# Two products of the next pair among the output steps of a pair, in a hand-ordered convolution and SwiGLU kernel

## The chip, the cores and the metric

The kernel runs on one core of one Trainium2 chip. The metric is the device time of one execution in microseconds (us), as the median of the executions shown. The profiler's trace of one further execution stands beside it, with times from the first to the last instruction (the span).

## The reference

The input `x` holds 8 sequences of 4096 tokens with 192 values each. First comes a causal convolution over 7 tokens, with one softmax-normalised set of 7 taps for each of 8 heads (24 values a head); then, token by token, an RMS norm and a gated feed-forward layer with 1536 hidden values, all in fp32:

```
out = einsum('hk,bskhg->bshg', softmax(weight), windows of x)   # lightweight_conv
rms = sqrt(mean(out * out) + 1e-6);  xn = out / rms * rms_g
g = xn @ w_gate;  silu = g / (1 + exp(-g));  val = xn @ w_val
result = (silu * val) @ w_out                                    # 32768 x 192
```

## The kernel before, in words

**Tiling.** The 32768 tokens are cut into 32 *pairs* of two tiles of 512 tokens. Pair 0 and pair 1 are made in a prologue with plain fp32 products (lines 881 and 1090), while weights are prepared. Pairs 2 to 31 run in a steady order that repeats once a pair; a *window* is one such repeat (the loop over `w` at the end of the kernel).

**Products.** The hidden values of a pair come from *products* (`product`, matmul at line 909). One product is six matmuls of 64 rows by 128 columns over 512 tokens: three parts of a split operand, each for the gate (array rows 0 to 63) and the value (rows 64 to 127) at once, so a product is three concurrent matmul couples. Left operands are pieces of the split weights, loaded from DRAM into a ring of 10 slots (`ring_load`, line 789, queue of SyncE); the right operands are five groups of split token sums. The 12 blocks of 128 hidden values are taken as 6 couples `j`, each with four cells a, b, c, d (two token tiles by two blocks), each cell a double bank of PSUM (gate and value). For `j` = 1 and 3 each cell gets three products of its own (named A, B, E with the cell: `Ab.1`). For `j` = 0, 2, 4, 5 a Winograd-like form needs 11 products (P1 to P7, Q1 to Q4) and sums in between. So a pair has 4x11 + 2x12 = 68 products.

**Emptying the banks.** The order is written out as words: engine letter (V VectorE, A ScalarE, G GpSimd, S the DMA queue of SyncE), act, index. `f1.j` copies cell a into a new bank b, `f3.j` copies c to SBUF (both line 674 on ScalarE, line 676 on VectorE), `f4.j` and `f5.j` add the copy to b (VectorE, line 980; f5 opens cell d). `ga` to `gd` take the SiLU of a gate bank (ScalarE, line 986), `ma` to `md` multiply by the value bank (VectorE, line 993) and so write the hidden values `ht`. A bank is free for another cell when both have read it. There are four double banks for everything.

**Output.** `h1.k` to `h4.k` are sums of hidden values in place (line 963, VectorE or GpSimd, SBUF to SBUF). An output step `oF.k` (form F of 1 to 7, k of 0 to 5; `step`, matmul at line 936) is a set of matmuls with tiles of 128 rows by 32 columns, in plain fp32. The 42 steps add into accumulators X (forms 1, 6, 5, 3), Y (2) and Z (7, 4), of one double bank each. `c1` copies X into Y, `s7` and `c2` copy Z and X to SBUF, `C22` and `C21` (line 1010) add X and Z to these copies, `T11`, `T12`, `T21`, `T22` (line 951) transpose into `o_sb`, and `Sst` stores it (line 1042). `C22` must read X before the steps of form 3 add to it; `T12` reads X after them.

**Next pairs, meanwhile.** `cv0` to `cv6` are the taps of a convolution (lines 440 to 444), `sq`, `red`, `pow`, `bc`, `mul` the norm (`mul` on GpSimd, line 494), `Spl`, `Sft`, `Sld` DMAs that put the result away, fetch it transposed and load the next tokens; `x1` to `x4` (line 831), `n` (ScalarE, line 674), `l` (line 817) and `d` (line 819) make the five groups of split operands (0 to 4) of the next pair.

**What sets the order.** `ORDER` holds the words of a window: `pN` lets TensorE take N further products or steps of the window's pair from `LINE`; a suffix `-` means the pair before, `+` and `++` the next and the one after. Every engine keeps its own queue in that order, and semaphores hold an instruction until what it reads is there, or its bank is free. `FIRST` is the window of pair 1, with the preparation of the split weights (`W`) in it. In the kernel before, `LINE` starts a pair with P1.0 P5.0 Ab.1 P6.0 Bb.1 Eb.1 P7.0 P3.0 Q2.0 P2.0 Q1.0 Q4.0, and all 42 output steps of a pair stand behind its 68 products and ahead of the next pair's first product; 15 of these steps stand at the start of the next window.

Of the kernel before, what the change touches and what calls it, by code (L numbers as in the profile page):

```python
# [20 lines left out]
def kernel(  # L21
# [55 lines left out]
        "a5 b5 c5 d5",  # L77
    )
    ORDER = (
# [14 lines left out]
    )  # L94
    FIRST = (
# [13 lines left out]
    )  # L109
    LINE = (  # L110
# [7 lines left out]
    )  # L118

    cst = ctx.enter_context(tc.tile_pool(name="cst", bufs=1))  # L120
# [1176 lines left out]
```

## Time and profile before

| what | value |
|---|---|
| time, median of 3 (lowest to highest) | 2484.42 us (2483.5 to 2485.6) |
| the profiled execution: its own time, its span | 2486.79 us, 2485.0 us |
| granted TensorE clock | 0.999 |
| VectorE, ScalarE, GpSimd busy | 2051.4, 993.1, 795.2 us |
| HBM read, written | 366.96 MB, 58.98 MB |

In the page's rows PE is the matmul part of TensorE and PEld its weight loads, DVE is VectorE, ACT ScalarE, POOL GpSimd, and SPq and ACTq are DMA queues. A group's row gives line, engine, operation, tiles and shape, count, then busy us and mean ns of one, then the engine's idle time before it with the releaser. A timeline row gives start, length, engine, line, operation, tiles and count; in square brackets stands the idle time before it and what ended it. A row of waits gives the total, the number and the longest.

### The profile page before, as it was taken

What the parts mean: (1) busy time and instruction counts of PE and PEld (TensorE: products, weight loads), DVE (VectorE), ACT (ScalarE), POOL (GpSimd) and SP (SyncE); (2) the same over time, 40 slices, a digit from 0 to 9 for tenths busy, and PEclk for the clock granted to TensorE, in tenths of its full rate; (3) what the DMA queues carried; (4) which work ended last, traced back from release to release, by engine and by line L of the source; (5) the groups of instructions that cost most, each with busy time, mean ns of one, the idle gap of its engine ahead of it and who ended that gap; (6) DMA issues with size and microseconds to landing.
All of it is one profiled execution on the core that took longest, in us unless ns stands there. A gap on an engine that the chain in (4) does not pass through costs nothing.

```text
span 2485.0 us, 69316 instructions
## 1 busy us (share of the span) xinstructions
PE 2464.4 (99%) x29152; PEld 1923.9 (77%) x29152; DVE 2051.4 (83%) x2614; ACT 993.1 (40%) x1405; POOL 795.2 (32%) x566
## 2 busy tenths in 40 slices
PE   8999999999999999999999999999999999999998
PEld 5547778878787777788887778877788777888876
DVE  8688888888888888888888888888887888888864
ACT  6443334434344434344334343333344343444332
POOL 0541332323332323323323324233423233333222
PEclk9999999999999999999999999999999999999999
DMA  6364678666677666787667786666776666776653
GB/s 151 60 205 127 167 182 211 178 172 168 170 193 198 179 165 171 175 204 185 182 161 175 179 206 185 173 164 172 187 200 185 171 168 170 199 192 186 161 159 92
DMA packets 716392, 430.55 MB, mean 173 GB/s; under 512 B 510330, under 2 KB 702386, under 8 KB 716082
## 3 DMA queue, kind: packets, MB, share of 16 engines
q1 hardware_dynamic: 712336, 425.21, 66.6%
q8 instruction: 230, 3.77, 0.6%
q10 hardware_dynamic: 3746, 0.92, 0.2%
q14 instruction: 80, 0.66, 0.1%
HBM read 366.96 MB, written 58.98 MB: 171 GB/s over the span
## 4 chain that ended last, share of the span: by engine, by line
PE 94%; DVE 2%; DMA 1%; SPq 1%; issue 1%; POOL 0%; ACT 0%; DVEq 0%; POOLq 0%
PE ps L909 57%; PE ps L936 35%; PE ps L881 2%; DMA ht<-in_moe_w_gate_dram 0%; SPq L237 0%; DVE ht L1108 0%; DVE ht L963 0%; SPq L153 0%; DVE y L444 0%; DMA xb<-xd 0%; DMA x<-in_x_dram 0%; DMA hs<-in_moe_w_out_dram 0%; DVE part L344 0%; DMA ring<-wd 0%; POOL part L335 0%
## 5 line engine op out<-in xcount | busy, mean ns | idle before, releaser
L909 PE MATMUL ps<-part,ring 64*128 64x512 f32 x12240 | 1434.0, 390 | 2.6 <-DVE ps L980 0.4
L909 PEld LDWEIGHTS ps<-part,ring 64*128 64x128 f32 x12240 | 1174.3, 184 | 255.3 <-DVE ps L980 32.3
L986 ACT ACTIVATE tt<-ps 128x512 f32<-128x512 f32 x744 | 436.1, 599 | 714.4 <-PE ps L909 636.0
L993 DVE TENSOR_TENSOR ht<-ps,tt 128x512 f32<-128x512 f32 x744 | 495.5, 686 | 195.6 <-ACT tt L986 192.4
L936 PE MATMUL ps<-ht,wo_sb 128*32 128x384 f32 (+2 forms) x7272 | 471.6, 380 | 0.8 <-POOL wo_sb L336 0.8
L963 POOL TENSOR_TENSOR ht<-ht 128x512 f32<-128x512 f32 x182 | 279.0, 1563 | 568.7 <-PE ps L936 568.7
L936 PE MATMUL ps<-ht,x 128*32 128x256 f32 (+2 forms) x6696 | 429.1, 379 | 1.3 <-DVE ht L963 1.3
L936 PEld LDWEIGHTS ps<-ht,wo_sb 128*32 128x32 f32 x7272 | 332.4, 110 | 102.4 <-DVE tt L831 9.4
L980 DVE TENSOR_TENSOR ps<-ps,tt 128x1024 f32<-128x1024 f32 x240 | 295.6, 1232 | 97.8 <-ACT tt L674 55.6
L936 PEld LDWEIGHTS ps<-ht,x 128*32 128x32 f32 x6696 | 299.0, 110 | 87.5 <-DVE ht L963 2.0
L444 DVE SCALAR_TENSOR_TENSOR y<-xh,tp,y 128x1536 f32<-128x1536 f32 x186 | 338.9, 1822 | 2.5 <-ACT y L440 2.3
L674 ACT COPY ps<-ps 128x1024 f32<-128x1024 f32 (+1 forms) x151 | 134.0, 887 | 478.6 <-PE ps L909 367.9
L963 POOL TENSOR_TENSOR hs<-ht 128x512 f32<-128x512 f32 x120 | 165.5, 1390 | 405.2 <-DVE ht L993 405.2
L473 POOL TENSOR_SCALAR r<-r 128x8 f32<-128x8 f32 x31 | 6.1, 198 | 484.5 <-DVE r L468 484.4
L674 ACT COPY tt<-ps 128x1024 f32<-128x1024 f32 (+1 forms) x152 | 121.6, 800 | 68.7 <-PE ps L936 57.9
L963 DVE TENSOR_TENSOR ht<-ht 128x512 f32<-128x512 f32 x190 | 132.5, 698 | 9.7 <-PE ps L936 6.4
L936 PE MATMUL ps<-hs,x 128*32 128x128 f32 (+2 forms) x2232 | 130.1, 379 | 0.0
L936 PEld LDWEIGHTS ps<-hs,x 128*32 128x32 f32 x2232 | 94.0, 110 | 30.7
L674 ACT CAST part<-tt 128x1024 fp32r<-128x1024 f32 x60 | 62.9, 1049 | 136.8 <-DVE tt L831 136.8
L963 DVE TENSOR_TENSOR ht<-hs,ht 128x512 f32<-128x512 f32 x156 | 106.7, 729 | 1.2 <-PE ps L936 0.6
L819 DVE SCALAR_TENSOR_TENSOR part<-part,xb 128x1024 fp32r<-128x1024 f32 x87 | 105.9, 1218 | 0.0
L817 POOL TENSOR_TENSOR part<-xb,part 128x1024 fp32r<-128x1024 f32 x29 | 96.6, 3329 | 0.0
(131 smaller groups left out, 1436.5 us busy)
## 6 DMA issues: line engine op xcount, KB each, us to landing
ring<-wd SPq DMA_DIRECT2D x1440, 192.0 KB
xb<-xd SPq DMA_DIRECT2D x60, 512.0 KB
xd<-xh SPq DMA_DIRECT2D x240, 96.0 KB
xh<-in_x_dram SPq DMA_DIRECT2D x192, 105.0 KB
xb<-xd SPq DMA_DIRECT2D x60, 256.0 KB
out_dram<-o_sb SPq DMA_DIRECT2D x126, 96.0 KB
out_dram<-o_sb SPq DMA_DIRECT2D x62, 128.0 KB
wd<-part SPq DMA_DIRECT2D x5, 1152.0 KB
```

What stands on the lines that cost most here:

```text
L444: nc.vector.scalar_tensor_tensor(out=y, in0=xk, scalar=w, in1=y, op0=ALU.mult, op1=ALU.add)
L473: nc.gpsimd.tensor_scalar(out=r, in0=r, scalar1=s / D, scalar2=s * 1e-6, op0=ALU.mult, op1=ALU.add)
L674: nc.scalar.copy(out=dst, in_=src)
L817: e.tensor_tensor(out=split_of(g, 1).bitcast(F32R), in0=src, in1=high, op=ALU.subtract)
L819: nc.vector.scalar_tensor_tensor(out=split_of(g, 2).bitcast(F32R), in0=high, scalar=1.0 + SPLIT, in1=src, op0=ALU.mult, op1=ALU.subtract,)
L881: nc.tensor.matmul(out=self.both(j, c)[:, h, :], lhsT=wf[HALF[h], k, 2 * HOME[j] + f, :], rhs=rb[HALF[h], k, g, :], start=(k == 0), stop=( ...
L909: nc.tensor.matmul(out=self.both(j, c)[:, h, :], lhsT=left[HALF[h]], rhs=right[HALF[h]], start=(first and q == 0), stop=True, skip_group_c ...
L936: nc.tensor.matmul(out=self.acc(b)[i * Q : (i + 1) * Q, at : at + n], lhsT=left, rhs=cols, start=fresh, stop=True, skip_group_check=True, ...
L963: engine[eng].tensor_tensor(out=dst, in0=a, in1=b, op=op)
L980: nc.vector.tensor_tensor(out=self.both(j, c), in0=self.both(j, "b"), in1=s5, op=ALU.add)
L986: nc.scalar.activation(out=tt[:, t, :], in_=self.both(j, c)[:, 0, :], func=AF.Silu)
L993: nc.vector.tensor_tensor(out=self.hv(j, "abcd".index(c)), in0=self.both(j, c)[:, 1, :], in1=tt[:, t, :], op=ALU.mult,)
```

## The change

Three strings of words are replaced; no instruction of the arithmetic is added or dropped. These are the last part of `LINE` and the seam of `ORDER` (a window's end and, in the next round, its start), cut to what is spoken of:

```diff
 LINE, first and last rows
-        "P1.0 P5.0 Ab.1 P6.0 Bb.1 Eb.1 P7.0 P3.0 Q2.0 P2.0 Q1.0 Q4.0 Aa.1 Ea.1 Ba.1 P4.0 Q3.0",
+        "P5.0 P1.0 P2.0 Q1.0 P6.0 Ab.1 Bb.1 Eb.1 P7.0 Q2.0 Aa.1 P3.0 Ea.1 Ba.1 P4.0 Q3.0 Q4.0",
...
-        "Q3.4 P4.4 Q4.4 Aa.3 P1.5 Ea.3 P5.5 P6.5 Ba.3 Q1.5 P2.5 P7.5 Q2.5 P3.5 P4.5 Q3.5 Q4.5",
+        "Q4.4 Q3.4 P4.4 P1.5 Aa.3 Ba.3 P5.5 P6.5 Ea.3 P2.5 Q1.5 P7.5 Q2.5 P3.5 Q3.5 Q4.5 P4.5",
...
-        "o3.1 o4.2 o4.1 o3.4 o3.3 o3.0 o3.5 o3.2",
+        "o5.5 o2.4 o3.3 o3.1 o3.0 o3.5 o3.2 o3.4",
 ORDER, start and end of a window
-        "p4- Vd.3 Vl.3 Gh4.0- Gh4.2- p3- Vl.4 Vh4.1- Gl.1 Vd.4 Vh4.3- Vd.2 Vh4.5- Vcv1+ VC22-",
-        "VT11- p8- Vcv2+ VT22- Vl.2 VC21- p1 Af1.0 VT12- VT21- p1 Af3.0 p1 Vcv3+ p1 Vf4.0 p2",
+        "p2 Vl.2 VC22- VT11- p3- Vd.4 VT22- VT21- Vcv3+ p3- Af1.0 Af3.0 VT12- p4 Aga.0 Vcv4+",
+        "Vf4.0 Vma.0 p2 Vcv5+ p1 Sst0.4- Sst0.2- Sst1.4- Agb.1 p5 Agc.0 Aga.1 Vmb.1 Vf5.0 p3",
+        "Vcv6+ Vma.1 Vmc.0 Agb.0 Agd.0 p2 Vmb.0 Asq+ Vmd.0 p3 Af1.2 Agc.3 Af3.2 p2 Vred+ p1",
...
-        "Vh4.4 Vd.0+ Vx4+ p8 An.3+ An.4+ As7 Ac2 An.2+ Acv0++ p5",
+        "An.2+ As7 p1 Ac2 Acv0++ Vh4.0 Vd.3+ Vd.2+ p11 Vh4.5 Vl.3+ Vh4.3 Vl.4+ Vcv1++ Vl.1+",
+        "Vcv2++ Vd.1+ p3 Gh4.1 VC21 Gh4.4 Gh4.2",
```

TensorE's order at the seam was: 42 steps of a pair, then P1.0 P5.0 Ab.1 P6.0 ... of the next. It is now: 36 steps, then P5.0 P1.0 of the next pair, then the six steps of form 3, then P2.0 Q1.0 P6.0 Ab.1 Bb.1 Eb.1 P7.0. On VectorE the seam is now C21, l.2, C22, T11, d.4, T22, T21, cv3, T12, cv4, f4.0, ma.0, cv5, mb.1, f5.0, cv6, ma.1, mc.0. Some words change engine: x3 and x4 and l.0 go from VectorE to GpSimd, l.1 from GpSimd to VectorE, f3.4 from VectorE to ScalarE; of the h sums, h1.0, h3.2, h4.1 and h4.4 go to GpSimd and h1.4, h3.0, h3.4 and h4.0 to VectorE (counts on GpSimd before and now: h1 4 and 4, h2 1 and 1, h3 4 and 3, h4 2 and 3). The last sums of form 4 (h4.1, h4.4, h4.2) stand on GpSimd behind the 36th step. Stores and loads on SyncE's queue move with the rest, and the words between the seams are shuffled. `FIRST` gets more of the next pair's words: four d and four l ahead of h1.5, where there were three and two on VectorE, and cv2 of pair 3 ahead of C22.

39 rows, old and new, of tables (FIRST, LINE, ORDER) are left out of this document.

## The prediction

> **What bounds the kernel now.** The page first: which engine is full, and at what clock.
>
> ```profile
> PE 2464.4 (99%) x29152; PEld 1923.9 (77%) x29152; DVE 2051.4 (83%) x2614; ACT 993.1 (40%) x1405; POOL 795.2 (32%) x566
> PEclk9999999999999999999999999999999999999999
> PE 94%; DVE 2%; DMA 1%; SPq 1%; issue 1%; POOL 0%; ACT 0%; DVEq 0%; POOLq 0%
> ```
>
> TensorE is busy all the time and is the chain that ends last, so time goes only by what it does or by stalls that its busy time hides. The chain in order of time shows the period (start, length):
>
> ```profile
> 906.25 39.51 PE ps L909 x342
> 945.76 27.44 PE ps L936 x337
> 981.46 39.58 PE ps L909 x337
> 1056.73 39.50 PE ps L909 x342
> ```
>
> From 981.46 to 1056.73 is 75.27 us for a pair: 27.44 for the 42 output steps (0.653 each), 47.8 for the 68 products. What a product costs undisturbed, and where one is disturbed, stands in the weight loads (PEld timeline of one pair; six loads are a product; a row ends where the loads pause):
>
> ```profile
> 1048.40 0.53 PEld L909 LDWEIGHTS ps<-part,ring 64*128 64x128 f32 x6 [0.20 <-issue]
> 1049.22 3.30 PEld L909 LDWEIGHTS ps<-part,ring 64*128 64x128 f32 x30 [0.29 <-DVE o_sb L951]
> 1052.98 3.29 PEld L909 LDWEIGHTS ps<-part,ring 64*128 64x128 f32 x30 [0.46 <-DVE ps L980]
> 1056.70 7.40 PEld L909 LDWEIGHTS ps<-part,ring 64*128 64x128 f32 x66 [0.43 <-issue]
> 1064.25 16.87 PEld L909 LDWEIGHTS ps<-part,ring 64*128 64x128 f32 x150
> 1081.35 7.34 PEld L909 LDWEIGHTS ps<-part,ring 64*128 64x128 f32 x66 [0.23 <-DVE ps L980]
> 1088.85 4.65 PEld L909 LDWEIGHTS ps<-part,ring 64*128 64x128 f32 x42 [0.15 <-ACT ps L674]
> 1093.89 1.91 PEld L909 LDWEIGHTS ps<-part,ring 64*128 64x128 f32 x18 [0.39 <-DVE ps L980]
> 1096.16 1.02 PEld L936 LDWEIGHTS ps<-ht,wo_sb 128*32 128x32 f32 x22 [0.35 <-DVE tt L831]
> ```
>
> The 66 loads from 1056.70 are 11 products in 7.55 us up to the next row, the 66 from 1081.35 in 7.50: 0.68 each. So 68 products need 46.24 and 1.5 us a pair is lost. Row by row, start to start less 0.68 a product: 0.14 (P1.0), 0.36 (five products), 0.32 (five), 0.07, 0.10 (25 products), 0.02, 0.28 (seven), 0.23 (three): 1.52. A load that comes late also leaves the first matmul behind it uncovered: in the last row of products 0.11 of the 0.23 is this. By the order of the words the pauses are: P1.0 (the switch from output steps), P5.0 waiting for T12 (0.13), P7.0 for f4.0 (0.30), Q4.0 for f5.0 (0.28; the row names "issue", but the 0.43 ends as f5.0 does), P6.2 for f1.2 (0.06), P7.4 for f4.4 (0.10), P6.5 for f1.5 (0.02), P4.5 for f5.5 (0.27). That is 1.16 in seven waits; 0.23 is the two switches' part inside the products (0.11 ahead of P1.0's second couple, 0.12 ahead of o1.0); 0.13 is jitter after late loads. The totals over the run agree that such waits recur in each pair:
>
> ```profile
> PEld ps L909 <- DVE ps L980: 32.3, 90, 0.5
> PEld ps L909 <- DVE o_sb L951: 8.7, 30, 0.3
> PEld ps L909 <- DMA ring<-wd: 1.0, 2, 0.7
> ```
>
> 90 waits on f4 and f5 in 30 pairs are three a pair. The ring's loads are late twice in the run; SyncE's queue is reordered (its stores stand later, its loads stay behind the products that free a slot), and I cost that at nothing: the cover is ten slots, about seven us of products.
>
> **The change part by part.** *Taken away.* Durations for the sums:
>
> ```profile
> L980 DVE TENSOR_TENSOR ps<-ps,tt 128x1024 f32<-128x1024 f32 x240 | 295.6, 1232 | 97.8 <-ACT tt L674 55.6 <-PE ps L909 29.1
> L993 DVE TENSOR_TENSOR ht<-ps,tt 128x512 f32<-128x512 f32 x744 | 495.5, 686 | 195.6 <-ACT tt L986 192.4
> L444 DVE SCALAR_TENSOR_TENSOR y<-xh,tp,y 128x1536 f32<-128x1536 f32 x186 | 338.9, 1822 | 2.5 <-ACT y L440 2.3
> L676 DVE COPY tt<-ps 128x1024 f32<-128x1024 f32 x30 | 36.4, 1214 | 0.0
> ```
>
> T12 must follow the last step of form 3. Now P5.0 and P1.0 use banks that T12 does not free, and it frees one only for Ab.1, four products after those steps: 0.13 goes. f4.0 starts when P6.0 is through and takes 1.23; between P6.0 and P7.0 stood two products (1.36), now three (2.04): 0.30 late becomes 0.38 early. f5.0 stands on VectorE behind f4.0, a tap (1.82) and a product of banks (0.69), now one more of these; between P7.0 and its user stood four products, now five before P4.0: 0.28 late becomes some 0.2 early. f3.4 leaves VectorE (1.21), so f4.4's 0.10 goes. f1.2's 0.06 goes (its user P6.2 stands one product further back).
>
> *Stays.* f5.5 still has two products (1.36) between P7.5 and its user (now Q3.5), and takes 1.23 and the hand-overs: 0.27 stays. f1.5's 0.02 goes and f1.4 gets the tight place that f1.2 had: 0.04.
>
> *Added wait.* From f4.0 to ma.1 VectorE has no pause: f4.0, ma.0, cv5, mb.1, f5.0, cv6, ma.1 are 2x1.23 + 3x0.69 + 2x1.82 = 8.2, less some 0.08 of overlap at each join, 7.7; it starts 0.9 after P6.0, and P1.2, 13 products (8.84) after P6.0, needs ma.1's bank 0.15 earlier: 0.1 late at P1.2. Queued behind it on TensorE is the whole pair. So waits of 1.16 become 0.27 + 0.04 + 0.10 = 0.41, jitter with fewer late loads 0.13 becomes 0.08: **0.80 us a pair comes out**.
>
> *Added work.* TensorE now changes four times a pair between 64x128 and 128x32 tiles, not twice. The price of one more pair of switches from pair 1, where single steps stand among products of line 881 (timelines of PE, then of PEld):
>
> ```profile
> 149.69 10.57 PE L881 MATMUL ps<-xb,part 64*128 64x512 f32 x48
> 160.19 0.86 PE L936 MATMUL ps<-ht,wo_sb 128*32 128x384 f32 x12
> 160.98 10.63 PE L881 MATMUL ps<-xb,part 64*128 64x512 f32 x48
> ...
> 150.22 0.19 PEld L881 LDWEIGHTS ps<-xb,part 64*128 64x128 f32 x2 [0.23 <-issue]
> 156.66 0.19 PEld L881 LDWEIGHTS ps<-xb,part 64*128 64x128 f32 x2 [0.24 <-issue]
> ```
>
> The two load rows are the first and the last of 16 in even steps: 6.44/15 = 0.429 a couple, 24 couples 10.30. From 149.69 to 160.98 is 11.29, so the step took 0.99 instead of 0.65: **0.34** for both switches. Upper end, from the rows above: 0.20 pause ahead of P1.0's load, 0.14 in P1.0, 0.12 ahead of o1.0: 0.46. Lower end nothing, if the next tiles' loads slip in beside the running matmuls. I take 0.36, near the measured single step. The Trainium skill, TensorEngine Tiling (Array Packing), section Tiling Modes, speaks against the change here: changing the mode, not just the tile, drains TensorE. The trace agrees with 0.34 a pair of switches; the page has no price, so the sum stays.
>
> *Moved to GpSimd* (x3, x4, l.0; h4.1, h4.4, h4.2). Now the same engine's rows and VectorE's beside them:
>
> ```profile
> 1097.22 1.29 POOL L963 TENSOR_TENSOR ht<-hs,ht 128x512 f32<-128x512 f32 x1 [2.70 <-PE ps L936]
> 1116.68 4.05 POOL L963 TENSOR_TENSOR ht<-ht 128x512 f32<-128x512 f32 x2 [18.16 <-PE ps L936]
> 1120.68 3.36 POOL L817 TENSOR_TENSOR part<-xb,part 128x1024 fp32r<-128x1024 f32 x1
> ...
> 1117.71 1.87 DVE L444 SCALAR_TENSOR_TENSOR y<-xh,tp,y 128x1536 f32<-128x1536 f32 x1
> 1120.05 1.75 DVE L817 TENSOR_TENSOR part<-xb,part 128x1024 fp32r<-128x1024 f32 x1
> ```
>
> A sum on GpSimd takes 1.29 alone; the second of the two from 1116.68 took 2.8, as if it began when the tap of 1117.71 ended at 1119.58 (1.29 more is 1120.87; it ended at 1120.73). So of two SBUF-to-SBUF operations the later waits for the earlier. In the new order h4.4 may start when o2.4 is through, about as P5.0 starts (0). l.2 runs until 0.35; h4.4 ends near 1.5; d.4, waiting by then, takes its 1.22 until 2.6; h4.2 ends near 3.8. o3.2 stands two products, a switch and four steps after 0: 1.36 + 0.1 + 2.61 = 4.1, and wants h4.2 by 3.9. Just early: nothing. x3, x4 and l.0 have ten us and more until P5.0.
>
> *Once only.* In `FIRST` VectorE has one d and two l more, less two x (net some 2.3 us), ahead of h3.5, and cv2 ahead of C22: +2.5 us at the first seam. At the end
>
> ```profile
> 2478.28 4.14 ACTq L1042 DMA_DIRECT2D out_dram<-o_sb  x6
> ```
>
> six stores issue behind the last transposes; T21 and T22 now stand ahead of the last steps, so three are issued earlier: -1.5 us with C22 late by 0.4 there. Together +1.
>
> **Sum:** 30 x (0.80 - 0.36) = 13.2 less 1.0 is 12.2 us. From the profiled execution's 2486.8 (span 2485.0 and 1.8 around it) that gives 2474.6; it stands 2.4 above the median of 2484.4, so 2472.2 as a median; I say **2472.5**.
>
> **Rivals.** *Switches eat it* (no change). With 0.46 a switch, P1.2 later by 0.2 and f5.0 still late by 0.1, 0.80 - 0.46 - 0.30 leaves 0.04 a pair: 1.2 us less 1.0, 2484. For it: each of those slacks is a difference of long sums. Against: 0.34 was measured on several single steps.
>
> *GpSimd late at o3.2* (slower). If h4.4 and h4.2 each take 2.8, as one did next to a tap, h4.2 ends at 5.7 and o3.2, with the next pair's products behind it, is 1.8 late in each pair: 30 x 1.8 - 12.2 = 42 us, 2526. It decides from h4.2 ending after 3.9, that is from a mean of over 1.9 for the two. For it: only 0.1 to spare, and d.4, cv3 are SBUF-to-SBUF. Against: d.4 is waiting before h4.4 ends, so only d.4 stands between. A small miss of 0.3 costs 9 us and gives 2481. The Trainium skill, SBUF — State Buffer, section Who interferes with whom, has this rule: the first to start holds the shared ports for its whole instruction, the other fully blocks. The trace agrees (2.8 against 1.29, ended by the tap's end).
>
> *Switches free*: 30 x 0.80 = 24, 2461.
>
> *The products cannot stand ahead*: if C21, which frees their bank, were late, P5.0 would wait. C21 needs o4.2, two steps (1.3) ahead, and takes 0.55: 0.4 to spare; part of the first rival.
>
> **How the numbers follow.** Chances: forecast (2464 to 2479) 0.70; switches free or nearly 0.06; no gain (2479 to 2489) 0.13; GpSimd late 0.11. The range 2462 to 2483 holds the first two, the small miss and most of no gain. A measurement of this kernel tells about 0.2% (5 us) from no change: faster than 2479.4 has 0.74, within 0.2% 0.14, slower 0.12.
>
> **What would show it.** Right: a period near 74.8 in the chain; waits on line 980 down from 90 to some 30, on line 951 gone; two pauses with "issue" more in each pair. Wrong: GpSimd named as the releaser ahead of line 936, or the loads of P1.2, P4.0 late by more than 0.2.

## The result and the profile after

The kernel after took 2477.26 us (median of 10, 2475.57 to 2480.92), the kernel before beside it 2485.02 (median of 10, 2483.5 to 2487.81): ratio 0.9967, 95% interval 0.9959 to 0.9975, so 0.33% faster by the ratio, 7.8 us by the medians. The profiled executions have spans of 2476.6 and 2485.0. Line numbers after are one higher than before (product 910, step 937, f4 and f5 981).

First the page of the kernel after (busy time and chain by engine). TensorE is still full and still the chain that ends last:

```profile
PE 2454.1 (99%) x29152; PEld 1896.0 (77%) x29152; DVE 2020.8 (82%) x2526; ACT 1018.0 (41%) x1435; POOL 836.2 (34%) x624
PE 92%; DVE 4%; DMA 2%; issue 1%; ACT 1%; POOL 0%; SPq 0%; DVEq 0%; POOLq 0%; ACTq 0%
```

Next the chain of the kernel after, in order of time (start, length): the steps of pairs 2 and 3, a whole pair in the middle, and the last pair.

```profile
271.71 23.54 PE ps L937 x288
...
346.45 23.54 PE ps L937 x288
...
594.15 1.58 PE ps L910 x12
595.73 4.04 PE ps L937 x48
599.77 45.55 PE ps L910 x396
645.33 23.54 PE ps L937 x288
668.87 1.58 PE ps L910 x12
...
2443.11 23.54 PE ps L937 x288
```

The seam is seen at once: 36 steps (23.54), two products (1.58), the six steps of form 3 (4.04), 66 products. From 594.15 to 668.87 is 74.72, as from 271.71 to 346.45 (74.74); before it was 75.23 in most pairs. The same rows of the kernel before, for pairs 3 and 31:

```profile
343.06 27.44 PE ps L936 x337
...
2450.31 27.46 PE ps L936 x337
```

These four starts and the spans split the 8.4 us. Up to pair 3's steps the kernel after has **lost 3.4** (346.45 against 343.06). From there to pair 31 it **gains 10.6** (2096.7 against 2107.3; 28 pairs at 0.49 would be 13.7, so some 3 are lost again in single pairs). After that it **gains 1.2** (33.5 against 34.7 to the end of the span).

What holds the weight loads, first in one pair (PEld timeline of the kernel after, the pair whose steps of form 3 start at 1046.06), then in the waits over the run (total us, number, longest):

```profile
1044.48 1.23 PEld L910 LDWEIGHTS ps<-part,ring 64*128 64x128 f32 x12 [0.20 <-issue]
1046.06 3.84 PEld L937 LDWEIGHTS ps<-ht,wo_sb 128*32 128x32 f32 x72 [0.36 <-DVE o_sb L952]
1050.10 10.07 PEld L910 LDWEIGHTS ps<-part,ring 64*128 64x128 f32 x90 [0.20 <-issue]
1060.40 16.91 PEld L910 LDWEIGHTS ps<-part,ring 64*128 64x128 f32 x150 [0.23 <-DVE ht L994]
1077.46 15.53 PEld L910 LDWEIGHTS ps<-part,ring 64*128 64x128 f32 x138 [0.15 <-ACT ps L675]
1093.39 1.91 PEld L910 LDWEIGHTS ps<-part,ring 64*128 64x128 f32 x18 [0.39 <-DVE ps L981]
```

```profile
PEld ps L910 <- DVE ps L981: 12.0, 29, 0.6
PEld ps L910 <- issue: 11.7, 59, 0.2
PEld ps L937 <- DVE o_sb L952: 9.7, 27, 0.4
PEld ps L910 <- DVE ht L994: 6.7, 29, 0.3
PEld ps L910 <- DMA ring<-wd: 4.5, 6, 1.4
PEld ps L937 <- DVE ht L964: 3.1, 1, 3.1
PEld ps L937 <- DVE tt L1011: 2.2, 3, 1.6
```

One wait a pair on f4 and f5 is left of three (29 for 90), that of f5.5 at Q3.5. The 59 pauses with "issue" are the two changes from steps to products. The change the other way, 0.36 at o3.3, stands under the name of line 952: T11 ends 0.05 ahead of it, but reads another bank, and C22, for which o3.3 must wait, ended 0.6 ahead. P1.2 waits for ma.1 (line 994). Of the last three rows, the late loads of the ring are not in the forecast; the longest waits of the other two (3.1 and 1.6) belong to the first seam, for which it had 2.5 in all.

### The profile page after: what moved, and what is told of

The parts are those of the page before. It is cut to its first block, busy times and chain, and to the rows that moved or that the text cites. A ratio compares the mean times of both kernels' runs of the same rounds, so it can differ in the third digit from the quotient of the medians.

```text
span 2476.6 us, 69229 instructions
## 1 busy us (share of the span) xinstructions
PE 2454.1 (99%) x29152; PEld 1896.0 (77%) x29152; DVE 2020.8 (82%) x2526; ACT 1018.0 (41%) x1435; POOL 836.2 (34%) x624
## 4 chain that ended last, share of the span: by engine, by line
PE 92%; DVE 4%; DMA 2%; issue 1%; ACT 1%; POOL 0%; SPq 0%; DVEq 0%; POOLq 0%; ACTq 0%
PE ps L910 54%; PE ps L937 35%; PE ps L882 2%; DMA xb<-xd 1%; DMA ring<-wd 1%; DVE y L445 0%; DVE ht L1109 0%; PE ps L408 0%; DVE ht L994 0%; DVE ps L981 0%; PE ps L528 0%; DVE part L345 0%; DVE part L330 0%; DVE ht L964 0%; ACT part L675 0%
## 5 line engine op out<-in xcount | busy, mean ns | idle before, releaser
L910 PEld LDWEIGHTS ps<-part,ring 64*128 64x128 f32 x12240 | 1151.3, 184 | 258.4 <-DVE ps L981 12.0
L937 PE MATMUL ps<-ht,x 128*32 128x384 f32 (+2 forms) x6696 | 440.3, 380 | 2.9 <-DVE ht L964 2.9
L675 ACT COPY tt<-ps 128x384 f32<-128x384 f32 (+1 forms) x182 | 151.7, 834 | 225.0 <-PE ps L937 161.0
L964 POOL TENSOR_TENSOR hs<-ht 128x512 f32<-128x512 f32 x120 | 155.4, 1295 | 262.0 <-DVE ht L994 262.0
L937 PE MATMUL ps<-hs,x 128*32 128x128 f32 (+2 forms) x2232 | 161.2, 379 | 0.0
L937 PEld LDWEIGHTS ps<-hs,x 128*32 128x32 f32 x2232 | 106.8, 110 | 29.7
L820 DVE SCALAR_TENSOR_TENSOR part<-part,xb 128x1024 fp32r<-128x1024 f32 x87 | 120.1, 1380 | 0.0
L818 POOL TENSOR_TENSOR part<-xb,part 128x1024 fp32r<-128x1024 f32 x29 | 69.6, 2401 | 122.3 <-PE ps L910 86.1
L495 POOL TENSOR_TENSOR xh<-y,s 128x1536 f32<-128x1536 f32 x30 | 89.9, 2997 | 15.3 <-DVE s L487 7.7
```

What stands on the lines that cost most here:

```text
L495: e.tensor_tensor(out=yn[p].rearrange("p a t -> p t a"), in0=y, in1=ss[:].rearrange("p (t o) -> p t o", o=1).to_broadcast([P, TB, GS]), op ...
L675: nc.scalar.copy(out=dst, in_=src)
L818: e.tensor_tensor(out=split_of(g, 1).bitcast(F32R), in0=src, in1=high, op=ALU.subtract)
L820: nc.vector.scalar_tensor_tensor(out=split_of(g, 2).bitcast(F32R), in0=high, scalar=1.0 + SPLIT, in1=src, op0=ALU.mult, op1=ALU.subtract,)
L910: nc.tensor.matmul(out=self.both(j, c)[:, h, :], lhsT=left[HALF[h]], rhs=right[HALF[h]], start=(first and q == 0), stop=True, skip_group_c ...
L937: nc.tensor.matmul(out=self.acc(b)[i * Q : (i + 1) * Q, at : at + n], lhsT=left, rhs=cols, start=fresh, stop=True, skip_group_check=True, ...
```

## The experiments

Each was run beside the kernel before; "period" is the usual distance of pairs in the chain.

**The interleaving alone.** In the kernel before, C21 goes ahead and P1.0 and P5.0 stand ahead of the last five steps:

```diff
-VT11- p8- Vcv2+ VT22- Vl.2 VC21- p1 Af1.0 VT12- VT21- p1 Af3.0 p1 Vcv3+
+VT11- p2- VC21- p1- p2 p5- Vcv2+ VT22- Vl.2 Af1.0 VT12- VT21- Af3.0 p1 Vcv3+
-o3.1 o4.2 o4.1 o3.4 (LINE)
+o4.2 o4.1 o3.1 o3.4
```

> The kernel before with the interleaving alone: P1.0 and P5.0 of the next pair ahead of the last five steps of form 3 (o4.2, o4.1 and C21 are put ahead of these), all else in the old order. Theory (the interleaving is only a means; the gain comes from the products P2.0, Q1.0 that stand between the last steps and Ab.1, and between P6.0 and P7.0): the extra pair of tile switches costs 0.36 a pair; T12's wait moves from P5.0 (0.13) to Ab.1, which now stands directly behind the steps, at about 0.8; f4.0, still behind T12, T21 and cv3, is later against P7.0 by another 0.4 to 0.6. Sum +1.4 to +1.6 us a pair, 2485 + 45 = about 2530. Rival (standing among the steps is what brings the gain): T12's 0.13 goes, at most the switch is added: 2481 to 2492.

2528.63, ratio 1.0172 (1.0158 to 1.0186): 43 us slower, as the theory had it. Its waits:

```profile
PEld ps L909 <- DVE ps L980: 40.9, 90, 0.8
PEld ps L909 <- DVE o_sb L951: 31.4, 30, 1.0
PE ps L909 <- DVE o_sb L951: 23.3, 30, 0.8
```

T12 (line 951) now stops the matmuls themselves for 0.8 in each pair, and f4.0 is later. In the old order, standing among the steps brings nothing.

**The interleaving undone** in the kernel after, all else kept:

```diff
-p2 Vl.2 VC22- VT11- p3- Vd.4 VT22- VT21- Vcv3+ p3- Af1.0
+Vl.2 VC22- VT11- p3- Vd.4 VT22- VT21- Vcv3+ p3- p2 Af1.0
```

> The kernel after with one thing undone: P5.0 and P1.0 stand behind the six steps of form 3 again, all other words and the order of the other products as they are. Theory (what the two products buy is cover): a pair of switches goes (-0.32), but o3.3 comes 1.4 earlier and waits for C22, which ended 0.6 ahead of it (0.8 late, with a late load's 0.1 and what follows 0.9 to 1.3), o3.2 for GpSimd's h4.2 (0.3 to 0.4), and P2.0 stands directly behind P1.0 and must wait for f1.0 (1.0 long, and f1.0 reads what P2.0 adds to: 1.1 to 1.4). Sum +2.0 to +2.7 us a pair: 2477 + 60 to 80, about 2550. Rival (the gain comes from the rest of the reordering, the interleaving costs its switches): 2466 to 2470.

2553.61, ratio 1.0277 (1.0263 to 1.0291); period 77.21. The waits name the three things that the two products covered: f1.0 (line 675) ahead of P2.0, C22 (1011) ahead of o3.3, GpSimd's h4.2 ahead of o3.2.

```profile
PE ps L910 <- ACT ps L675: 34.1, 30, 1.1
PE ps L937 <- DVE tt L1011: 31.4, 30, 3.2
...
PEld ps L937 <- POOL ht L964: 10.2, 29, 0.4
```

So neither half of the change pays alone in these two arrangements: the new order needs the cover, and the cover needs the new order.

**A third pair of switches.** o1.0 of each pair goes ahead of its last product, P4.5:

```diff
-Q3.5 Q4.5 P4.5 o1.0 o7.0 (LINE)
+Q3.5 Q4.5 o1.0 P4.5 o7.0
```

> The kernel after with o1.0 taken one place forward, ahead of P4.5, so that TensorE changes its tiles six times a pair instead of four; no other word is moved. Theory: one more pair of switches costs what pair 1's single steps and the seam showed, 0.34 to 0.38 us: 30 x 0.36 = 11, so 2477.3 + 11 = about 2488. Rival one (switches nearly free, the other waits filled in for them): 2477 to 2479. Rival two (0.46, the upper bound): 2491.

2486.1, ratio 1.0002 (0.9993 to 1.0011). The chain gives the price without the run's irregular pairs:

```profile
270.84 22.89 PE ps L937 x280
...
345.91 22.89 PE ps L937 x280
```

75.07 against 74.74: **0.33 us** a pair of switches (30 are 9.9). The waits that recur in each pair are as they were (line 981 12.1 us in 30, line 994 6.9 in 29), and the new change to steps is the same pause of 0.36, here under the name of line 994 (10.9 us in 30). The whole gain of the change is as large as one more of them.

**P7.0 back to its old distance** behind P6.0:

```diff
-Ab.1 Bb.1 Eb.1 P7.0 (LINE)
+Ab.1 Bb.1 P7.0 Eb.1
```

> The kernel after with P7.0 put back to two products behind P6.0 (ahead of Eb.1), as in the kernel before. Theory: f4.0 ended 0.5 ahead of P7.0, 0.68 less makes it 0.15 to 0.2 late, with a late load's 0.1 together 0.25 to 0.3 a pair; P1.2's wait of 0.11 goes with it, since TensorE comes there later. Sum +0.15 to +0.25: 2477.3 + 6 = about 2483. Rival (f4.0's place was not what cost): 2477.

2481.32, ratio 0.9986 (0.9977 to 0.9995); the waits on line 981 are 26.3 us in 61 instead of 12.0 in 29, and the one on ma.1 has gone. The period is 0.18 longer, of the 0.49 gained in each pair; by the ratios this one place in the order is worth 4.7 us of 8.2.

**The first seam mended.** Three splits of pair 2 go behind h4.0, the last loads of pair 3 ahead of the ring's start, its first taps ahead of h4.2 (FIRST):

```diff
-... Sld.1++ Vl.2+ p1 ... Gl.0+ Vd.0+ An.4+ Vl.4+ p1 Vh1.5
+... Sld.1++ p1 ... Gl.0+ An.4+ p1 Vh1.5
-Vh4.0 R p1 As7 p1 Sld.5++ p2 Sld.6++ p1 Sld.7++ p2 Ac2 p1 Vh4.3
+Vh4.0 Vl.2+ Vd.0+ Sld.5++ Sld.6++ Sld.7++ R Vl.4+ p1 As7 p4 p2 Ac2 Acv0++ p1 Vh4.3 Vcv1++ Vcv2++
-p9 Vh4.2 Acv0++ p2 Vh4.1 p1 Vcv1++ p1 VC21 p1 Vh4.4 Vcv2++
+p9 Vh4.2 p2 Vh4.1 p2 VC21 p1 Vh4.4
```

> The kernel after with the first window's words alone changed: l.2, d.0 and l.4 of pair 2 stand behind h4.0 instead of ahead of h1.5, the last loads of pair 3 ahead of the ring's start, and cv0, cv1, cv2 of pair 3 ahead of h4.2. Theory: the one-time loss of the kernel after lies in VectorE's backlog at the first seam, 2.9 us ahead of o7.5 (h3.5), 0.5 ahead of P5.0 (C21) and 1.4 ahead of o3.3 (C22), and goes: -4.8, about 2472.5. Rival (the work is only shifted and the ring's start or the loads of pair 3 are late next): 2477.

2469.61, ratio 0.9933 (0.9919 to 0.9946). Pair 2's steps start at 266.13 in its chain instead of 271.71: 5.6 for the 4.8 expected. Another 3 us lie in single pairs: from there to pair 31 its chain takes 2168.3 where the kernel after takes 2171.4, and late loads of the ring hold it for 1.5 us in three, not 4.5 in six. No word of the later windows was changed, so why these pairs are less late is not shown; a second profile of the kernel after has 3.3 us in five. What had stood in the way is plain in VectorE's timeline of the kernel after: h1.5 and h3.5 come last, without a gap, behind l.2, d.0 and l.4 of pair 2 (lines 818 and 820) and md.5. These are the last four of the rows:

```profile
196.91 2.81 DVE L820 SCALAR_TENSOR_TENSOR part<-part,ring 128x1024 fp32r<-128x1024 f32 x1
199.65 1.21 DVE L818 TENSOR_TENSOR part<-tt,part 128x1024 fp32r<-128x1024 f32 x1
200.78 0.68 DVE L964 TENSOR_TENSOR hs<-ht 128x512 f32<-128x512 f32 x1
201.49 0.69 DVE L964 TENSOR_TENSOR ht<-ht 128x512 f32<-128x512 f32 x1
```

At the same seam P5.0 and o3.3 waited for C21 and C22 (line 1011; PEld timeline of the kernel after):

```profile
219.24 1.22 PEld L910 LDWEIGHTS ps<-part,ring 64*128 64x128 f32 x12 [0.66 <-DVE tt L1011]
222.04 3.84 PEld L937 LDWEIGHTS ps<-ht,wo_sb 128*32 128x32 f32 x72 [1.57 <-DVE tt L1011]
```

**An eleventh slot for the ring,** in the unused tail of another tile. The reason is in SyncE's queue. First the kernel before (timeline of the queue), then the kernel after, at the same products:

```profile
1083.90 4.21 SPq L789 DMA_DIRECT2D ring<-wd  x6
1088.17 0.90 SPq L645 DMA_DIRECT2D xb<-xd  x2
```

```profile
1084.09 0.42 SPq L646 DMA_DIRECT2D xb<-xd  x1
1084.62 3.04 SPq L790 DMA_DIRECT2D ring<-wd  x5
1087.71 0.42 SPq L646 DMA_DIRECT2D xb<-xd  x1
```

Before, the loads for Q1.5 and the products behind it were issued ahead of both fetches of 512 KB; now one fetch stands ahead of them. Over all pairs the load for Q1.5 takes 3.0 us to land before (median) and 5.1 after, and its slack, the time from landing to the product's first matmul, falls from 3.1 to 0.85. The kernel before was not without tight places: the load for Bb.3 has a slack of about 1 there, and accounts for its late loads. In single pairs of the kernel after Q1.5's load is late (PEld timeline of one):

```profile
1015.53 0.53 PEld L910 LDWEIGHTS ps<-part,ring 64*128 64x128 f32 x6 [1.33 <-DMA ring<-wd]
```

```diff
-NSLOT = 10
+NSLOT = 11
-out=ring[0][:, slot, :]
+out=(ring[0][:, slot, :] if slot < 10 else xsplit[0][:, 8, 0 : KP * P])
-spc.tile([P, 8, T], F32, name="part0")
+spc.tile([P, 9, T], F32, name="part0")
... (the product reads its left operand from the same place)
```

> The kernel after with eleven slots in the weights' ring instead of ten (the eleventh in the tail of a tile that the prologue had used for weights); no word is moved. Theory: the irregular stalls of the kernel after (Q1.5 and P3.5 late by 0.5 to 1.2 in single pairs) are ring loads that stand on SyncE's queue behind the fetch of 512 KB; with one slot more each load is issued at least one product (0.68) earlier, the smallest slack rises from 0.04 to 0.7, these stalls go: -1.5 to -4 us, about 2474.5, with executions closer together than the 2475.6 to 2480.9 of the kernel after. Rival (the irregular stalls come from elsewhere, VectorE's and GpSimd's shared access or the fetch itself): 2477 and the same scatter.

2474.72 (2474.57 to 2475.94), ratio 0.9956 (0.9944 to 0.9969): 2.7 us better by the ratios, whose intervals overlap, and closer together. What the slot does to the loads is clear: Q1.5's now stands ahead of the fetch in each pair and takes 3.8 us to land, with a slack of 3.4, while the four behind the fetch keep their 4.5 to 5.0. Their smallest slack up to the weight load rose to 0.1 only, not to the 0.7 expected. One load of the ring was still late (0.6 us; with ten slots the waits list 4.5 in six), and only part of the irregular time, that of pairs longer than the usual period, went. The rest looks like this (timeline of ScalarE, then of PEld, in one such pair):

```profile
1312.59 1.05 ACT L675 CAST part<-xb 128x1024 fp32r<-128x1024 f32 x1 [0.69 <-DMA xb<-xd]
1313.54 1.08 ACT L987 ACTIVATE tt<-ps 128x512 f32<-128x512 f32 x2
```

```profile
1316.25 0.53 PEld L910 LDWEIGHTS ps<-part,part 64*128 64x128 f32 x6 [1.08 <-DVE ps L981]
```

The copy n.0 waits for the fetch; ga.3 is queued behind it on ScalarE, ma.3 behind that frees the bank which f5.5 opens, and Q3.5 waits for f5.5.

**Both together.** The last two edits in one kernel:

> The kernel after with the mended first window and the eleventh slot together. Theory: the two gains are of different places and add up: 2469.6 and another 1 to 3 us (ring loads that were late by 0.3 to 0.5 in pairs 5 and 16 of the mended seam's trace), about 2467.5. What stays are single pairs in which the fetch of 512 KB itself lands late and holds n.0, ga.3, ma.3 and so f5.5 (0.7 each). Rival (each of the two had the same irregular stalls taken out): 2469.6.

2468.9, ratio 0.9938 (0.9926 to 0.9951), not to be told from the mended seam alone: the slot's gain did not add up here. Pairs 7, 11 and 17 of its trace were late by 0.4 to 0.9, all three at Q3.5 through f5.5.

**The fetch earlier,** on top of both: the fetch (`Sft.0`, `Sft.1`) and pieces four and five (`Spl`) go three products forward, piece six one; piece seven stays.

```diff
-Spl.3+ p6 Spl.4+ Agc.1 p1 Af1.4 Spl.5+ Spl.6+ Spl.7+ ... Vf4.4 p4 Aga.4 Sft.0+ Sft.1+
+Spl.3+ p3 Spl.4+ p1 Spl.5+ p2 Spl.6+ Agc.1 p1 Af1.4 Spl.7+ ... Vf4.4 p1 Sft.0+ Sft.1+ p3 Aga.4
```

> As the mended first window with the eleventh slot, and in each pair the pieces put away four to seven and the fetch behind them stand three to four products earlier on SyncE's queue. Theory: the fetch lands some 2 us earlier, n.0 is no longer late ahead of ga.3 in single pairs, and the extra time of irregular pairs (2.6 us with eleven slots) falls under 1: about 2466. Rival (the loads that the fetch is put ahead of are late instead): 2468 to 2471.

2468.92, ratio 0.9936 (0.9923 to 0.9948): a miss. The irregular time of its profile was some 3 us, now from late loads of the ring, ahead of P3.4 and Q2.5 among others, and from h2.1, which stands behind x1 and x2 on VectorE and so behind the fetch's later part (x2's line waits 18.0 us in 15 for it, 5.9 in 7 without this edit). Q1.5's load stands behind the fetch again and takes 5.7 us to land. As its rival said, the fetch only hit other loads.

**n.0 behind ga.3,** with seam and slot:

```diff
-Vf4.5 An.0+ Aga.3 p3
+Vf4.5 Aga.3 An.0+ p3
```

> The mended first window with the eleventh slot, and one word more moved: n.0, ScalarE's copy that waits for the fetch, stands behind ga.3 instead of ahead of it, so that a late fetch no longer holds the bank that f5.5 opens. Theory: the 2.2 us of single pairs in which f5.5 was late by 0.4 to 0.75 go, nearly no irregular time is left: 2466.5 to 2467.5. Rival (l.0 and the sums behind it on GpSimd come 0.6 later in every pair, and h4.2, which has 0.3 to spare, is late at o3.2 by some 0.1): 2470 to 2472.

> The kernel after unchanged, on the same chip as the run beside it. Expected 2477 with executions some 3 to 5 us apart, so that the mended version's 2467 to 2469 can be set beside it directly.

2467.22 (2466.64 to 2469.07), ratio 0.9931 (0.9918 to 0.9943); the kernel after beside it 2476.47 (2475.91 to 2478.24), ratio 0.9969 (0.9958 to 0.998). The version beats both kernels, by 9 and 17 us. Its chain, pairs 2, 3 and 31:

```profile
265.44 23.54 PE ps L937 x288
...
340.16 23.54 PE ps L937 x288
...
2432.26 23.54 PE ps L937 x288
```

28 pairs at 74.72 are 2092.2, and 2432.26 less 340.16 is 2092.1: no irregular time is left in this execution. GpSimd's h4.2 was not late. Against seam and slot without n.0's move the ratios do not separate (0.9931 and 0.9938).

## Why the prediction was right

The sign was right and the time in the range; 2477.3 lies 4.8 above the 2472.5 named. In the spans 8.4 us came out where the sum had 12.2: about 2.4 more were lost at the first seam, 3.1 in single pairs and 0.3 at the end, and the usual pairs gave 1.5 more than forecast, so part of the misses cancelled. By its own steps:

- *Waits taken out, 0.80 a pair.* Right: the net gain and one pair of switches make 0.49 + 0.33 = 0.82. f4.0, f5.0 at Q4.0, f1.2, f4.4 and T12 are gone (P6.2 stands two products further behind P1.2 than before, not one), and the three waits named are there. Start to start in the PEld timeline, less 0.68 a product, they are 0.10 ahead of P1.2, 0.06 ahead of P6.4 and 0.29 ahead of Q3.5 (f5.5): 0.45 where 0.41 was named. P7.0's distance was shown to matter by putting it back. The 0.1 at P1.2 came out with luck. The sum's own terms, 0.9 + 7.7 = 8.6 against 8.84 - 0.15 = 8.69, leave ma.1 0.1 early. In the trace f4.0 begins 1.2 after P6.0's first weight load, because the tap cv4 ahead of it on VectorE ends only then, and from there to the end of ma.1 it takes 7.8 (medians of 30 pairs). One sign named for "right" did not come: the pauses with "issue" are 59 as before, not two a pair more. One of them now stands for the new change to products, but Q4.0's wait, which had borne that name, is gone, and the change to steps is named by line 952.
- *One more pair of switches, 0.36.* Right, 0.33 when a third pair is added. The price that spoke against the change is there, and it takes two fifths of what comes out. Net 0.49 a pair (75.23 to 74.74) against 0.44 forecast: 1.5 us better over 30 pairs.
- *GpSimd just early.* Right and nearly as tight as said (0.3 to spare for 0.1). In the kernel after its last two sums end at 1048.35 (timeline of GpSimd), and o3.2 starts 0.3 later by the trace:

```profile
1044.64 3.71 POOL L964 TENSOR_TENSOR ht<-ht 128x512 f32<-128x512 f32 x2 [1.10 <-PE ps L937]
```

  They took 3.71 where two alone would take 2.6; the steps taken 1.4 earlier made them late at once.
- *Once only, +1.0.* The term failed in its size at the start: +2.5 was named for the first seam. The trace has 2.9 ahead of o7.5, 0.5 ahead of P5.0, 1.2 ahead of o3.3 (the pauses less what the mended seam leaves there) and one extra switch: 4.9. The backlog ahead of h3.5 was seen (2.3 net), but d.0 took 2.81 beside GpSimd's l.0 (195.70 to 198.64) instead of 1.2; and cv1 and cv2, ahead of C21 and C22, made 1.7 more where the sum had next to nothing. The end gave 1.2 of the 1.5 named.
- *SyncE's queue, nothing.* This step failed. It spoke of stores and loads and not of the fetch, which had moved ahead of five loads. "About seven us" is near the median time from a load's issue to its use (7.1), but Q1.5's has 5.7, and 5.1 of them pass until it lands; in single pairs it lands too late. Over the 28 pairs the kernel after took 3.9 us more than 28 of its usual periods (74.74), the kernel before 0.8 more (75.23). In other profiles the same 28 pairs, 2096.7 here, took 2094.5 (the kernel after again), 2093.6 (seam), 2094.7 (slot), 2094.4 (both) and 2092.1 (both and n.0's new place). So the stalls differ between executions, and one profile of each does not tell what each edit took of them.

Of the rivals, switches free and products that cannot stand ahead are out by the runs; "switches eat it" had the right mechanism at too high a price. Not settled: why the fetch lands late in some pairs and not in others (4.6 to 7.4 us for the first of a pair in the kernel after); the runs only show whom it hits.

## What to carry to other kernels

When work is moved between engines' queues, follow the DMA queue too and take the smallest slack of its loads, not the mean depth of the buffer: a big transfer put ahead of small ones takes theirs. Price a change of tile shape first (0.33 us here) and ask which waits its cover removes; neither the interleaving nor the reordering paid alone. And read the start of the loop apart from its steady part: the first window lost some 5 us, against a net gain of 7.8.

## What the runs showed of the hardware

- A small load (192 KB) issued behind a 512 KB fetch on the same queue took 4.5 to 5.1 us to land (medians of five loads in the kernel after, the worst 7.6), where the same five took 3.0 to 3.8 issued ahead of it in the kernel before. The two loads that stood behind the fetches in the kernel before took 6.0 and 6.8 there, and had 25 us to spare; Q1.5's load, put ahead of the fetch by the eleventh slot, fell from 5.1 to 3.8. The Trainium skill, DMA: Bandwidth & Descriptors, section Two DMAs through the same engine are not ordered, says that within one queue of one DMA engine the descriptors start in order. The traces show landings and not starts; they fit: in the pair shown the fetch landed at 1088.8 and the first load behind it at 1089.3.
- A change from 64x128 to 128x32 tiles and one back cost 0.33 us together, measured by adding a third pair of them in each pair (75.07 against 74.74); around single steps in the prologue it was 0.34.
